# Attention scores by rows in two of every three units, with the reciprocal sums applied per head after the output projection

## The chip, the cores and the metric

The kernel runs on one core of a Trainium2 chip. The metric is the device time of one execution in microseconds (us). The median of 3 runs of the kernel before is 1313.21 us (1313.07 to 1313.99). All times inside the kernel come from one profiled execution.

The engines are called as in the profile: PE multiplies matrices, PEld is its load of the stationary operand, DVE is the vector engine, ACT computes the exponential and the GELU, POOL and SP do little arithmetic and issue transfers. PSUM is the memory into which PE writes; a bank holds 512 float32 values in each of 128 partitions.

## The reference, cut to what matters

The block is an attention with cached keys and values, followed by a gated MLP, each behind a modulated layer norm. The change touches the attention:

```python
q = (x @ wq).reshape(B, Sq, Hq, Dh).transpose(0, 2, 1, 3)   # Sq 2048, Hq 32, Dh 128
k = jnp.repeat(k_cache, rep, axis=1)                       # 8 key heads, rep 4
v = jnp.repeat(v_cache, rep, axis=1)
scores = jnp.einsum('bhqd,bhkd->bhqk', q, k) * Dh ** (-0.5)
p = softmax(scores, axis=-1)
o = jnp.einsum('bhqk,bhkd->bhqd', p, v)
return o.transpose(0, 2, 1, 3).reshape(B, Sq, Hq * Dh) @ wo  # wo: 4096 x 512
```

The result is scaled by a gate and added to x; a second layer norm and the MLP follow, which multiplies one half of its hidden values with a 2048 x 2048 spatial projection of the other half.

## The kernel before, in words

The attention is cut into 128 units. Unit u belongs to group g = u // 16 (one key head with its four query heads) and to query tile j = u % 16 (128 queries). The main loop runs over iterations `it`, and each iteration over eight slots. In iteration `it` the program computes the scores of unit `it` (`qk`), the product of P and V of an earlier unit (`pv_at` says in which iteration), and the output projection of a still earlier one (`wo_at`). The instructions are written out in this order by hand, so each engine runs its own in the order of the loop. Work that has a due time is put in by `at(iteration, slot, function)`: it comes first in its slot. `fill` holds the matmuls of the query projection, four in each iteration, in slots 0 to 3.

There are two ways to compute a unit.

- **By columns**: `qk` makes the scores transposed, keys in the partitions, so that the exponential lands in `pT` as PV needs it. `pv` takes 128 x 128 pieces of `pT` as the stationary operand and V with a column of ones as the moving one (129 columns, 64 matmuls in a unit). The column of ones yields the sum of the row; DVE takes its reciprocal and multiplies (`onorm`, L1091 and L1092), and a transposing transfer on SP turns the result into `oT` (L1100).
- **By rows** (`by_rows(u)`): the queries are in the partitions. ACT's exponential sums up the row as it goes (`accum_out`, L1012). `turn_rows` adds the two half sums, takes the reciprocal, multiplies the 128 x 2048 rows of P by it on DVE (L1050), and issues a transposing transfer on SP that writes them into `pT` (L1051), one for each of the four heads. `pv_rows` then has V as the stationary operand and 512 columns of `pT` as the moving one (16 matmuls in a unit), and its result is `oT` after one copy (L1068).

Before the change the even units from 8 (`TURN_A`) to 124 are computed by rows, 59 of them; their PV comes three iterations after their scores, and that of the 69 others one iteration after. There is one PV in each iteration, except in iteration 9, which has none, and iteration 127, which has two.

`wo_proj` multiplies the four heads of `oT` with `wo` in one PSUM bank, four matmuls that accumulate, and DVE adds the bank to `xacc` (L1125; in the first group a copy, L1123). In the last group (units 112 to 127) DVE then multiplies by the gate (L1130), adds x (L1131) and takes the statistics (L697, L698) of the second layer norm. `ln2` puts the rest in: the square root on POOL in the next iteration, the normalisation `xn` and its transposing transfer `xnT` on SP in slot 4, and the modulated `hT` (L1156) in slot 5 of the iteration after that. From iteration 128 on the MLP's first matmuls fill the slots (`zrun`), and DVE takes the statistics of their GELU (`z2_stats`, L1312) and normalises it (`z2_norm`); the spatial matmuls (L1456) need all of that.

PSUM has two banks each under the names `o_ps` (PV) and `misc` (query projection and output projection) and two pairs under `s_ps` (scores). A bank is taken again when the engine that empties it is done. `pT` has three homes (`pT0`, `pT1`, `wsp`), given out by the table before the loop. The rows of P lie in six buffers (`pn`), taken in turn. For each group g from 1 on, SP loads the keys with a transposing transfer in iteration 16 (g - 1) + 11, slot 5; POOL loads V and the two weights after it has seen that the transposes of a certain row unit have landed (`after_rows`).

Of the kernel before, what the change touches and what calls it, by code (L numbers as in the profile page):

```python
# [15 lines left out]
P = 128  # L16
# [559 lines left out]
def kernel(  # L576
# [118 lines left out]
    def ln_stats(mv, j, src):  # L695
        st = stat.tile([P, 1, nc.vector.BN_STATS_DIM], FP32, name="bnst")
        nc.vector.bn_stats(out=st[:, 0, :], in_=src)  # L697
        nc.vector.bn_aggr(out=mv[:, j, :], in_=st[:])  # L698
# [266 lines left out]

    TURN_A, TURN_B = 2 * CT, NU - 2

    def by_rows(u):
        return TURN_A <= u < TURN_B and u % 2 == 0

    def pv_at(u):
        return u + 3 if by_rows(u) else u + 1

    def wo_at(u):
        return pv_at(u) + (3 if u < TURN_B - CT else 2)
# [11 lines left out]
    def at(it, slot, fn):  # L987
        later.setdefault((it, slot), []).append(fn)

    def qk(u, i):  # L990
# [10 lines left out]
        if by_rows(u):  # L1001
            hh, half = divmod(i, 2)
            for c in range(2):
                k0 = (2 * half + c) * 512
                nc.tensor.matmul(  # L1005
                    s_ps[:, c * 512 : (c + 1) * 512],
                    lhsT=qTs[b][:, hh, jj * P : (jj + 1) * P],
                    rhs=groups[g]["kT"][:, k0 : k0 + 512],
                    start=True,
                    stop=True,  # L1010
                )
            nc.scalar.activation(  # L1012
                out=rows_of(u, hh)[:, half * HK : (half + 1) * HK],
                in_=s_ps[:],
                func=ACT.Exp,
                scale=inv_sqrt_dh,
                accum_out=rsums[u][:, i : i + 1],
            )
            if half == 1:
                at(*divmod(u * NSLOT + i + 2, NSLOT), lambda: turn_rows(u, hh))  # L1020
            return
        for h in range(2):
            kt = 2 * i + h
# [12 lines left out]
        )  # L1036

    def rows_of(u, hh):
        return pn[((u - TURN_A) // 2 * REP + hh) % len(pn)][:, 0:SK]

    def turn_rows(u, hh):
        c0 = u * REP + hh
        rs, rinv = rsums[u], rall[:, c0 : c0 + 1]
        tot = stat.tile([P, 1], FP32, name="tot")
        nc.vector.tensor_tensor(  # L1045
            out=tot[:], in0=rs[:, 2 * hh : 2 * hh + 1], in1=rs[:, 2 * hh + 1 : 2 * hh + 2], op=ALU.add
        )
        nc.vector.reciprocal(out=rinv, in_=tot[:])  # L1048
        rows = rows_of(u, hh)
        nc.vector.tensor_scalar(out=rows, in0=rows, scalar1=rinv, scalar2=None, op0=ALU.mult)  # L1050
        nc.sync.dma_start_transpose(out=pTs[u][:, :, hh * P : (hh + 1) * P], in_=rows)  # L1051

    def pv_rows(u, i, n):

# [48 lines left out]

    def wo_proj(u):
        g, j = divmod(u, NT)
        ps = {}

        def mm(hh):
            if hh == 0:
                ps[0] = bank("misc")  # L1110
            X_ps = ps[0]
            nc.tensor.matmul(  # L1112
                X_ps[:],
                lhsT=oTs[u][:, hh, :],
                rhs=groups[g]["wo"][:, hh, :],
                start=(hh == 0),
                stop=(hh == REP - 1),
            )
            if hh < REP - 1:
                return  # L1120
            if g == 0:
                xaccs[j] = late.tile([P, D], FP32, name=f"xacc{j}", bufs=1)
                nc.vector.tensor_copy(out=xaccs[j][:], in_=X_ps[:])  # L1123
            else:
                nc.vector.tensor_tensor(  # L1125
                    out=xaccs[j][:], in0=X_ps[:], in1=xaccs[j][:], op=ALU.add
                )
            if g == HKV - 1:
                xa = xaccs[j]
                nc.vector.tensor_tensor(out=xa[:], in0=xa[:], in1=ga_rows[:], op=ALU.mult)  # L1130
                nc.vector.tensor_tensor(  # L1131
                    out=x_sb[:, j, :], in0=xa[:], in1=x_sb[:, j, :], op=ALU.add
                )
                ln_stats(mv2, j, x_sb[:, j, :])

        return [lambda hh=hh: mm(hh) for hh in range(REP)]

# [127 lines left out]
    for g in range(1, HKV):  # L1265
        it = (g - 1) * NT
        at(it + 11, 5, lambda g=g: load_k(g))
        loads = (
            lambda g=g: load_v(g),
            lambda g=g: load_wq(g, nc.gpsimd),  # L1270
            lambda g=g: load_wo(g, nc.gpsimd),
        )
        for k, load in enumerate(loads):
            if g == 1:
                at(5, 0, load)
                continue
            u = next(u for u in range(it + 4 + 2 * k, NU) if by_rows(u))
            at(u + 1, 5, lambda u=u: after_rows(u))
            at(u + 1, 5, load)

# [92 lines left out]
    for it in range(NU + 6):  # L1373
# [3 lines left out]
        elif it == NU:  # L1377
            free_a.close()
            z2p = fast.enter_context(tc.tile_pool(name="z2p", bufs=1))
            zs["z2"] = z2p.tile([P, NT, FH], BF16, name="z2")  # L1380
        pvs = [u for u in (it - 5, it - 3, it - 1) if 0 <= u < NU and pv_at(u) == it]
        wos = [u for u in range(max(it - 6, 0), min(it - 2, NU)) if wo_at(u) == it]
        wf = [fn for u in wos for fn in wo_proj(u)]
        for i in range(NSLOT):
            for fn in later.pop((it, i), []):
# [190 lines left out]
```

## Time and profile before

| what | value |
|---|---|
| median of 3 runs | 1313.21 us |
| profiled execution, span from first to last instruction | 1311.5 us |
| granted PE clock, mean | 0.999 |
| score matmuls by columns (L1024) and by rows (L1005) | 1104 and 944 |
| PV matmuls by columns (L1080) and by rows (L1059) | 4416 and 944 |
| transfers: row transposes (L1051), oT (L1100) | 236 and 69 |
| POOL waits in `seen` (L1258) | 18 |

The time of a run has about 1.7 us around the span. A page of the profile lists the busy time of each engine, the span in 40 slices of 32.8 us with the busy share in tenths, the chain of work that ended last followed back through its releasers, and groups of instructions with their count, busy time, mean duration in ns and the idle time of their engine just before them. An answer of the trace by windows gives the busy time of each engine in a stretch, with the number of instructions behind it. Mean durations of matmuls are from start to the modelled end; since they are pipelined, what one costs is the distance from start to start.

### The profile page before, as it was taken

What the parts mean: (1) busy time and instruction counts of PE and PEld (TensorE: products, weight loads), DVE (VectorE), ACT (ScalarE), POOL (GpSimd) and SP (SyncE); (2) the same over time, 40 slices, a digit from 0 to 9 for tenths busy, and PEclk for the clock granted to TensorE, in tenths of its full rate; (3) what the DMA queues carried; (4) which work ended last, traced back from release to release, by engine and by line L of the source; (5) the groups of instructions that cost most, each with busy time, mean ns of one, the idle gap of its engine ahead of it and who ended that gap; (6) DMA issues with size and microseconds to landing.
All of it is one profiled execution on the core that took longest, in us unless ns stands there. A gap on an engine that the chain in (4) does not pass through costs nothing.

```text
span 1311.5 us, 24369 instructions
## 1 busy us (share of the span) xinstructions
PE 1303.8 (99%) x9527; PEld 736.9 (56%) x9527; DVE 689.5 (53%) x1693; ACT 1113.0 (85%) x1533; POOL 59.4 (5%) x115
## 2 busy tenths in 40 slices
PE   9999999999999999999999999999999999999998
PEld 5665555555555555555555555555555555644445
DVE  5644455444454544444445454444445588784444
ACT  7899999999999999999999999999999999550000
POOL 1200000000000000000000000000000011120000
PEclk9999999999999999999999999999999999999999
DMA  6669778877897677867886778668876688364300
GB/s 181 154 97 157 130 128 154 158 118 133 158 166 149 121 144 155 144 125 140 160 169 122 133 157 156 125 127 153 175 143 125 118 140 144 103 133 96 82 21 27
DMA packets 607723, 174.45 MB, mean 133 GB/s; under 512 B 597264, under 2 KB 603664, under 8 KB 607600
## 3 DMA queue, kind: packets, MB, share of 16 engines
q1 hardware_dynamic: 600576, 153.67, 64.9%
q0 software_dynamic: 4432, 16.91, 4.1%
q10 hardware_dynamic: 2592, 2.23, 0.5%
q8 instruction: 77, 1.26, 0.4%
q14 instruction: 46, 0.38, 0.1%
HBM read 21.89 MB, written 2.10 MB: 18 GB/s over the span
## 4 chain that ended last, share of the span: by engine, by line
PE 96%; DVE 2%; DMA 1%; POOL 0%; issue 0%; ACT 0%; DVEq 0%; POOLq 0%
PE o_ps L1080 19%; PE s_ps L1024 18%; PE s_ps L1005 16%; PE o_ps L1059 16%; PE misc L1112 8%; PE misc L945 8%; PE misc L1456 7%; PE s_ps L1290 1%; PE o_ps L1477 1%; DVE stz L1312 1%; PE s_ps L1477 1%; DMA xnT<-xn 0%; DMA wmod_a<-in_w_mod_dram 0%; DVE z L686 0%; POOL rstd_lnz L682 0%; PE misc L855 0%
## 5 line engine op out<-in xcount | busy, mean ns | idle before, releaser
L1031 ACT ACTIVATE pT<-s_ps 128x1024 bf16<-128x1024 f32 x552 | 561.1, 1025 | 30.7 <-PE s_ps L1024 8.7
L1080 PEld LDWEIGHTS <-pT 128*128 128x128 bf16 x4416 | 295.3, 98 | 128.9
L1080 PE MATMUL o_ps<-v,pT 128*128 128x129 bf16 x4416 | 339.7, 220 | 0.0
L1024 PE MATMUL s_ps<-qT,kT 128*128 128x512 bf16 x1104 | 328.1, 379 | 0.3 <-ACT pT L1031 0.2
L1005 PE MATMUL s_ps<-kT,qT 128*128 128x512 bf16 x944 | 280.7, 379 | 0.0
L1012 ACT ACTIVATE win_sb<-s_ps 128x1024 bf16<-128x1024 f32 x238 | 243.7, 1025 | 3.5
L1112 PE MATMUL misc<-wo_g,oT 128*128 128x512 bf16 x512 | 194.0, 379 | 0.0
L945 PE MATMUL misc<-hT,wq_g 128*128 128x512 bf16 (+2 forms) x520 | 187.0, 371 | 0.1
L1024 PEld LDWEIGHTS <-kT 128*128 128x128 bf16 x1104 | 107.3, 98 | 114.9 <-issue 2.3
L1012 ACT ACTIVATE pn<-s_ps 128x1024 bf16<-128x1024 f32 x156 | 159.6, 1024 | 2.0 <-ACT wmod_a L1012 0.3
L1059 PEld LDWEIGHTS <-v 128*128 128x128 bf16 x944 | 92.4, 98 | 111.4
L956 DVE CAST qT<-misc 128x512 bf16<-128x512 f32 x125 | 85.7, 686 | 122.8 <-PE misc L945 122.8
L1068 DVE CAST oT<-o_ps 128x512 bf16<-128x512 f32 x59 | 40.8, 692 | 194.9 <-PE o_ps L1059 194.9
L1059 PE MATMUL o_ps<-wsp,v 128*128 128x512 bf16 x480 | 142.1, 379 | 0.0
L1059 PE MATMUL o_ps<-pT,v 128*128 128x512 bf16 x464 | 138.0, 379 | 0.0
L1005 PEld LDWEIGHTS <-qT 128*128 128x128 bf16 x944 | 92.2, 98 | 61.6
L1045 DVE TENSOR_TENSOR tot<-rs 128x1 f32<-128x1 f32 x236 | 36.4, 154 | 127.1 <-ACT win_sb L1012 84.8
L1456 PE MATMUL misc<-wsp,z 128*128 128x512 bf16 (+2 forms) x560 | 101.4, 336 | 0.2
L1050 DVE TENSOR_SCALAR win_sb<-win_sb,rall 128x2048 bf16<-128x2048 bf16 x119 | 89.7, 753 | 4.4 <-DVE rall L1048 0.3
L1012 ACT ACTIVATE wmod_a<-s_ps 128x1024 bf16<-128x1024 f32 x78 | 79.9, 1025 | 0.0
L1456 PEld LDWEIGHTS <-z 128*128 128x128 bf16 x560 | 50.5, 98 | 49.4 <-DVE z L686 1.6
L1125 DVE TENSOR_TENSOR xacc<-misc,xacc 128x512 f32<-128x512 f32 x112 | 76.2, 680 | 0.0
(110 smaller groups left out, 824.1 us busy)
## 6 DMA issues: line engine op xcount, KB each, us to landing
v<-in_A_v_cache_dram POOLq DMA_DIRECT2D x7, 512.0 KB, 6.6
wq_g<-in_A_wq_dram POOLq DMA_DIRECT2D x7, 512.0 KB, 3.9
wo_g<-in_A_wo_dram POOLq DMA_DIRECT2D x7, 512.0 KB, 4.5
wsp<-in_w_mod_dram POOLq DMA_DIRECT2D x1, 2048.0 KB, 9.1
out_dram<-yout ACTq DMA_DIRECT2D x16, 128.0 KB, 1.7
win_sb<-in_B_w_in_dram POOLq DMA_DIRECT2D x1, 1792.0 KB, 8.0
x_sb<-in_A_x_dram SPq DMA_DIRECT2D x3, 512.0 KB, 6.1
oT<-onorm SPq DMA_TRANSPOSE x69, 2.8
```

Of the source, the lines that this page charges most:

```text
L945: nc.tensor.matmul(ps[0][:, o0 : o0 + n], lhsT=wqs[g][:, dt, hh * DH : (hh + 1) * DH], rhs=hTs[ch][:, dt, c0 : c0 + n], start=(dt == 0), s ...
L956: nc.vector.tensor_copy(out=dst, in_=src)
L1005: nc.tensor.matmul(s_ps[:, c * 512 : (c + 1) * 512], lhsT=qTs[b][:, hh, jj * P : (jj + 1) * P], rhs=groups[g]["kT"][:, k0 : k0 + 512], sta ...
L1012: nc.scalar.activation(out=rows_of(u, hh)[:, half * HK : (half + 1) * HK], in_=s_ps[:], func=ACT.Exp, scale=inv_sqrt_dh, accum_out=rsums[u ...
L1024: nc.tensor.matmul(s_ps[:, h * 512 : (h + 1) * 512].rearrange("p (r q) -> p r q", r=REP), lhsT=groups[g]["kT"][:, kt * P : (kt + 1) * P], ...
L1031: nc.scalar.activation(out=pTs[u][:, 2 * i : 2 * i + 2, :], in_=s_ps[:].rearrange("p (k q) -> p k q", k=2), func=ACT.Exp, scale=inv_sqrt_dh,)
L1050: nc.vector.tensor_scalar(out=rows, in0=rows, scalar1=rinv, scalar2=None, op0=ALU.mult)
L1059: nc.tensor.matmul(o_pss[u][:], lhsT=groups[g]["v1"][:, kt, 0:DH], rhs=pTs[u][:, kt, :], start=(kt == 0), stop=(kt == NKT - 1),)
L1080: nc.tensor.matmul(o_ps[:, hh % 2, 0 : DH + 1], lhsT=pTs[u][:, kt, hh * P : (hh + 1) * P], rhs=groups[g]["v1"][:, kt, 0 : DH + 1], start=( ...
L1112: nc.tensor.matmul(X_ps[:], lhsT=oTs[u][:, hh, :], rhs=groups[g]["wo"][:, hh, :], start=(hh == 0), stop=(hh == REP - 1),)
L1125: nc.vector.tensor_tensor(out=xaccs[j][:], in0=X_ps[:], in1=xaccs[j][:], op=ALU.add)
L1456: nc.tensor.matmul(g_ps[:, :n], lhsT=z2[:, st, f * P : (f + 1) * P], rhs=wsp[t][:, st, c0 : c0 + n], start=(st == 0), stop=(st == NT - 1 a ...
```

## The change

Two of every three units from 8 to 125 are computed by rows, 79 in place of 59. With `(u - 8) % 3` the remainders 0 and 1 are by rows; their PV comes 2 and 3 iterations after their scores, that of remainder 2, by columns, 1 iteration after. There is still one PV in each iteration (none in 9, two in 127).

The rows of P are no longer multiplied by the reciprocal. They are turned as they are, one slot earlier than before (`i + 1` for `i + 2`), and the transfer is issued ahead of the sum and the reciprocal, which stay.

The reciprocals are applied to the projected output. For a row unit each of the four heads gets a bank of its own in `wo_proj`, with one matmul that starts and stops, and DVE adds the bank times the head's reciprocal to `xacc` (`scalar_tensor_tensor`; in the first group's first head a `tensor_scalar`). A column unit keeps one bank and one addition. The unit after whose transposes V and the weights are loaded must now be the second row unit of a pair.

```diff
--- before.py
+++ after.py
@@ -965,11 +965,15 @@
 
     TURN_A, TURN_B = 2 * CT, NU - 2
 
+    LAGS = (2, 3, 1)
+
     def by_rows(u):
-        return TURN_A <= u < TURN_B and u % 2 == 0
+        return TURN_A <= u < TURN_B and (u - TURN_A) % len(LAGS) < len(LAGS) - 1
+
+    row_units = [u for u in range(NU) if by_rows(u)]
 
     def pv_at(u):
-        return u + 3 if by_rows(u) else u + 1
+        return u + (LAGS[(u - TURN_A) % len(LAGS)] if by_rows(u) else 1)
 
     def wo_at(u):
         return pv_at(u) + (3 if u < TURN_B - CT else 2)
@@ -1017,7 +1021,7 @@
                 accum_out=rsums[u][:, i : i + 1],
             )
             if half == 1:
-                at(*divmod(u * NSLOT + i + 2, NSLOT), lambda: turn_rows(u, hh))
+                at(*divmod(u * NSLOT + i + 1, NSLOT), lambda: turn_rows(u, hh))
             return
         for h in range(2):
             kt = 2 * i + h
@@ -1036,19 +1040,19 @@
         )
 
     def rows_of(u, hh):
-        return pn[((u - TURN_A) // 2 * REP + hh) % len(pn)][:, 0:SK]
+        return pn[(row_units.index(u) * REP + hh) % len(pn)][:, 0:SK]
 
     def turn_rows(u, hh):
         c0 = u * REP + hh
-        rs, rinv = rsums[u], rall[:, c0 : c0 + 1]
+        rs = rsums[u]
+        nc.sync.dma_start_transpose(
+            out=pTs[u][:, :, hh * P : (hh + 1) * P], in_=rows_of(u, hh)
+        )
         tot = stat.tile([P, 1], FP32, name="tot")
         nc.vector.tensor_tensor(
             out=tot[:], in0=rs[:, 2 * hh : 2 * hh + 1], in1=rs[:, 2 * hh + 1 : 2 * hh + 2], op=ALU.add
         )
-        nc.vector.reciprocal(out=rinv, in_=tot[:])
-        rows = rows_of(u, hh)
-        nc.vector.tensor_scalar(out=rows, in0=rows, scalar1=rinv, scalar2=None, op0=ALU.mult)
-        nc.sync.dma_start_transpose(out=pTs[u][:, :, hh * P : (hh + 1) * P], in_=rows)
+        nc.vector.reciprocal(out=rall[:, c0 : c0 + 1], in_=tot[:])
 
     def pv_rows(u, i, n):
 
@@ -1103,35 +1107,49 @@
 
     def wo_proj(u):
         g, j = divmod(u, NT)
+        each = by_rows(u)
         ps = {}
 
+        def into(first, X_ps, scale):
+            if first:
+                xaccs[j] = late.tile([P, D], FP32, name=f"xacc{j}", bufs=1)
+            xa = xaccs[j]
+            if scale is None and first:
+                nc.vector.tensor_copy(out=xa[:], in_=X_ps[:])
+            elif scale is None:
+                nc.vector.tensor_tensor(out=xa[:], in0=X_ps[:], in1=xa[:], op=ALU.add)
+            elif first:
+                nc.vector.tensor_scalar(
+                    out=xa[:], in0=X_ps[:], scalar1=scale, scalar2=None, op0=ALU.mult
+                )
+            else:
+                nc.vector.scalar_tensor_tensor(
+                    out=xa[:], in0=X_ps[:], scalar=scale, in1=xa[:], op0=ALU.mult, op1=ALU.add
+                )
+
         def mm(hh):
-            if hh == 0:
+            if hh == 0 or each:
                 ps[0] = bank("misc")
-            X_ps = ps[0]
             nc.tensor.matmul(
-                X_ps[:],
+                ps[0][:],
                 lhsT=oTs[u][:, hh, :],
                 rhs=groups[g]["wo"][:, hh, :],
-                start=(hh == 0),
-                stop=(hh == REP - 1),
-            )
-            if hh < REP - 1:
+                start=(hh == 0 or each),
+                stop=(hh == REP - 1 or each),
+            )
+            if each:
+                c0 = u * REP + hh
+                into(g == 0 and hh == 0, ps[0], rall[:, c0 : c0 + 1])
+            elif hh == REP - 1:
+                into(g == 0, ps[0], None)
+            if hh < REP - 1 or g < HKV - 1:
                 return
-            if g == 0:
-                xaccs[j] = late.tile([P, D], FP32, name=f"xacc{j}", bufs=1)
-                nc.vector.tensor_copy(out=xaccs[j][:], in_=X_ps[:])
-            else:
-                nc.vector.tensor_tensor(
-                    out=xaccs[j][:], in0=X_ps[:], in1=xaccs[j][:], op=ALU.add
-                )
-            if g == HKV - 1:
-                xa = xaccs[j]
-                nc.vector.tensor_tensor(out=xa[:], in0=xa[:], in1=ga_rows[:], op=ALU.mult)
-                nc.vector.tensor_tensor(
-                    out=x_sb[:, j, :], in0=xa[:], in1=x_sb[:, j, :], op=ALU.add
-                )
-                ln_stats(mv2, j, x_sb[:, j, :])
+            xa = xaccs[j]
+            nc.vector.tensor_tensor(out=xa[:], in0=xa[:], in1=ga_rows[:], op=ALU.mult)
+            nc.vector.tensor_tensor(
+                out=x_sb[:, j, :], in0=xa[:], in1=x_sb[:, j, :], op=ALU.add
+            )
+            ln_stats(mv2, j, x_sb[:, j, :])
 
         return [lambda hh=hh: mm(hh) for hh in range(REP)]
 
@@ -1274,7 +1292,7 @@
             if g == 1:
                 at(5, 0, load)
                 continue
-            u = next(u for u in range(it + 4 + 2 * k, NU) if by_rows(u))
+            u = next(u for u in range(it + 4 + 2 * k, NU) if by_rows(u) and not by_rows(u + 1))
             at(u + 1, 5, lambda u=u: after_rows(u))
             at(u + 1, 5, load)
 
@@ -1378,8 +1396,8 @@
             free_a.close()
             z2p = fast.enter_context(tc.tile_pool(name="z2p", bufs=1))
             zs["z2"] = z2p.tile([P, NT, FH], BF16, name="z2")
-        pvs = [u for u in (it - 5, it - 3, it - 1) if 0 <= u < NU and pv_at(u) == it]
-        wos = [u for u in range(max(it - 6, 0), min(it - 2, NU)) if wo_at(u) == it]
+        pvs = [u for u in range(max(it - 5, 0), min(it, NU)) if pv_at(u) == it]
+        wos = [u for u in range(max(it - 8, 0), min(it, NU)) if wo_at(u) == it]
         wf = [fn for u in wos for fn in wo_proj(u)]
         for i in range(NSLOT):
             for fn in later.pop((it, i), []):
```

## The prediction

> **What bounds the kernel now.** I read the page from the top: engine shares, then the tenths by slice, then the chain that ended last.
>
> ```profile
> PE 1303.8 (99%) x9527; PEld 736.9 (56%) x9527; DVE 689.5 (53%) x1693; ACT 1113.0 (85%) x1533; POOL 59.4 (5%) x115
> ...
> DVE  5644455444454544444445454444445588784444
> ...
> PE 96%; DVE 2%; DMA 1%; POOL 0%; issue 0%; ACT 0%; DVEq 0%; POOLq 0%
> ```
>
> The chain is PE from end to end. DVE sleeps half the time, except in slices 32 to 35 (1049 to 1180 us), where it is at 7 to 9 tenths. Both facts carry the forecast: the change takes a little from PE everywhere and gives DVE work just there.
>
> The windows view gives stretches of that last part and, first, two neighbouring iterations of the steady state (unit 68 scored by rows, unit 69 by columns). Its columns: length, then busy time of PE, PEld, DVE, ACT, POOL, clock, DMA share, GB/s.
>
> ```profile
> 601.38:610.18 8.80, 8.80 (x89) 5.97 (x88) 5.62 (x15) 8.71 (x16) 0.00 (x0) 1.00 0.43 81
> 610.18:618.82 8.64, 8.64 (x42) 3.92 (x41) 2.88 (x8) 8.11 (x10) 0.17 (x2) 1.00 0.97 178
> 1105.81:1114.62 8.81, 8.81 (x89) 5.98 (x88) 7.79 (x17) 8.22 (x9) 2.23 (x5) 1.00 0.78 111
> 1146.15:1184.30 38.15, 38.09 (x184) 17.80 (x182) 31.92 (x85) 21.67 (x22) 9.12 (x14) 1.00 0.65 125
> ```
>
> PE is full in all of them. An iteration costs 8.81 or 8.64 us according to the unit whose PV it runs, not the one that it scores: eight slots, each with two score matmuls, one projection matmul, and either eight 129-column matmuls (PV of a column unit) or two of 512 (PV of a row unit).
>
> **1. PE gains 3.2 us.** By the timeline, PE's slot is 1.101 us with column PV and 1.079 with row PV; eight slots differ by 0.173 us. Row units go from 59 to 79 (u from 8 to 125, two of three), so 20 iterations change. Rows scoring beside row PV, new, has the same five 512-column matmuls in a slot: 1.079. From iteration 13 to 123 column PV is in 55 before and 37 after: 18 x 0.173 = 3.1; iteration 126 changes as well: 0.2. Iterations 8 to 12 lack their projections and are paced by ACT (1.005 us a slot by rows, 0.915 by columns, in the timeline at 81 to 98 us); one more of them is scored by rows. Slot by slot they come to 8.64 + 7.69 + 8.16 + 8.21 + 8.14 = 40.84 us, after 8.64 + 7.48 + 8.48 + 7.91 + 8.26 = 40.77 before: +0.1. ACT stays cover elsewhere: 2 x 8 x 1.005 + 8 x 0.915 = 23.4 us in three iterations, against PE's 8.81 + 2 x 8.63 = 26.1.
>
> On this term the Trainium skill, page "TensorE: Matmul & The Clock Gate", section "Back-to-back issue gap", speaks otherwise: streamed pairs of load and matmul go at about 81 ns for 128 columns and 131 ns for 512. By that the estimate is 64 x 81 - 16 x 131 = 3.1 us a unit, 62 us in all. The trace shows 56.6 and 215.8 ns, so it has no part in the sum.
>
> **2. The removed multiply gives nothing.** The page's groups have it (L1050, with two more of its kind, and below it the drain that term 4 uses):
>
> ```profile
> L1050 DVE TENSOR_SCALAR win_sb<-win_sb,rall 128x2048 bf16<-128x2048 bf16 x119 | 89.7, 753 | 4.4 <-DVE rall L1048 0.3
> ...
> L1125 DVE TENSOR_TENSOR xacc<-misc,xacc 128x512 f32<-128x512 f32 x112 | 76.2, 680 | 0.0
> ```
>
> 236 x 0.753 us go from DVE, hidden under PE: 0. The add and the reciprocal stay, one slot earlier. A transpose need not wait for them, only for ACT's second half.
>
> **3. More transposes, less time for them: +1.8 us (0 to 4).** Row transposes go from 236 to 316, those of oT from 69 to 49. The DMA view of 600 to 740 us:
>
> ```profile
> GB/s 33 24 200 208 185 28 170 157 180 187 100 176 205 211 176 32 172 205 211 173 172 34 201 217 173 24 38 200 210 166 28 41 200 210 120 75 44 202 212 172
> ...
> pT<-win_sb SPq DMA_TRANSPOSE x8, 4.4
> ...
> kT<-in_A_k_cache_dram SPq DMA_TRANSPOSE x1, 5.6
> ```
>
> One of 0.524 MB lands 4.4 us after issue; at the 205 to 210 GB/s of full slices, each next one 2.5 us later. Three iterations need 8 x 2.5 + 0.6 = 20.6 us of 26.1: enough. What is tight is the first row unit of a pair, whose PV now starts two iterations after its scores. From its own start, its heads are ready at 2.9, 5.1, 7.4 and 9.5 us; SP must first issue the column unit's oT, which waits for onorm (9.4) and takes 1.6, so the fourth issues at 11.1 and lands at 15.5. PV wants it at 8.81 + 8.63 + 0.43 = 17.87: slack 2.4. The V and weight loads start about at this unit's start, in idle DMA time; the V load before delayed a transpose by 0.9 to 1.8 us: covered. Not covered is a K transpose in SP's queue between the heads, in iterations 11, 59 and 107: it holds SP 2.2 to 3.6 us and pushes the landing to about 18.2. PE then stands 1.3 us in iteration 13 (short iterations before it) and 0.4 at the two others: 2.1, of which I take 1.8. In the last group an xnT transpose comes ahead of the second head in SP's queue and waits for DVE until 5.9: 0.8, inside the slack. The six row buffers cost no wait: the seventh head of a pair is written from 13.7 on, and the first, whose buffer it takes, has landed at 7.3.
>
> The Trainium skill, page "DMA: Bandwidth & Descriptors", section "Latency and other measured facts", gives 261 GB/s for a DMA transpose; a transpose would then take 2.0 us, an estimate, and this term would be 0. The full slices of this trace don't reach it.
>
> **4. Four drains for one.** A row unit's projection now fills a bank per head, each emptied by a scalar_tensor_tensor. The trace has none. Below: 0.68 us (L1125: same tiles without the scalar); above: two passes, 1.37. I take 0.70, nearest to L1125; 0.72 from start to start, as the chain below runs.
>
> In ordinary iterations this is free: misc has two banks, the third matmul needs the first drain two slots (2.16 us) later, and DVE has 3 us to spare. From unit 112 on a finish (L1130, L1131, statistics) follows; 3.0 us from drain to end:
>
> ```profile
> 1106.41 0.68 DVE L1125 TENSOR_TENSOR xacc<-misc,xacc 128x512 f32<-128x512 f32 x1
> 1107.12 0.69 DVE L1130 TENSOR_TENSOR xacc<-xacc,ga_rows 128x512 f32<-128x512 f32 x1
> 1107.85 0.69 DVE L1131 TENSOR_TENSOR x_sb<-xacc,x_sb 128x512 bf16<-128x512 f32 x1
> 1108.58 0.69 DVE L697 BATCH_NORM_STATS2 bnst<-x_sb 128x6 f32<-128x512 bf16 x1
> 1109.31 0.18 DVE L698 BATCH_NORM_AGGREGATE mv<-bnst 128x2 f32<-128x6 f32 x1
> ```
>
> With one projected unit per iteration DVE then has 9.0 us at most, 24.6 in three iterations of 26.1, and my schedule shows no bank late. It breaks in two places.
>
> **Iteration 126: +3.7 us (2.5 to 4.5).** It projects units 120 and 122, now both row units: eight banks in eight slots. DVE begins it with unit 121's drain and finish (0.82 to 3.82 us) and unit 125's sums (to 4.14), so the first drain ends at 4.83. The third matmul wants that bank at 3.02 and starts at 4.90: 1.88 lost. Unit 120's finish runs to 9.4, then 0.35 of xn and a drain to 10.44: the seventh matmul, due at 9.22, starts at 10.5: 1.28. After hT (0.9) and a drain to 12.05 the eighth, due at 11.58, starts at 12.1: 0.52. DVE's backlog of 4 us dies in iteration 127, where it idles 4.6 before.
>
> **Iterations 128 and 129: +2.7 us (1.5 to 4).** Units 123 and 125 bring three drains more each. The first three fit in an idle 1.6 us but for 0.4; the next, 3 x 0.72 = 2.2, find DVE with no gap from 1134.7 to 1160.7. That chain sets the end of this phase:
>
> ```profile
> DVE hT L1156 <- DMA xnT<-xn: 4.0, 1, 4.0
> ...
> PEld L1456 <- DVE z L686: 1.6, 4, 0.6
> ```
>
> These waits (1100 us to the end) say that DVE's one idle time there waits for a transpose which itself waits for DVE, and that PE's spatial matmuls already wait for the last normalised z. So 0.4 + 2.2 = 2.6, with a bank wait 2.7, goes into the end. PE loses about 2.5 in iteration 129 for the same banks; it runs beside and is not added.
>
> **Sum**, against the span of 1311.5 us: -3.2 + 1.8 + 3.7 + 2.7 = +5.0, so 1316.5. The median run is 1313.2, 1.7 above the span: 1318.2, rounded to **1318**.
>
> **Rivals.**
> - Faster: PE's gain stands and neither banks nor DMA cost anything, because DVE reaches the drains sooner than I schedule (it would have to regain 1.9 us by iteration 126): 1313.2 - 3.2 = 1310. For: DVE is 53% busy. Against: its four slices at 7 to 9. 0.12.
> - Half of it: one of the two places is absorbed or half as large: about 1313 to 1315. 0.18.
> - DMA as the bound: past 3.1 us a transpose (2.4 us of slack over four) each of 39 pairs stalls; at 3.3 that is 39 x 0.8 = 31 us: 1344. For: transposes, unlike before, queue through two iterations on end. Against: full slices at 205 GB/s. 0.05.
> - Dear drains: past 1.1 us each, the next query projection finds its bank late in all 79 units; at 1.37, 0.8 each, 63 us: 1376. 0.03.
> - Column PV paced by its weight loads: 98 ns each (PEld L1080 in the groups), so 64 x 98 - 16 x 215.8 ns = 2.8 us a unit, 56 in all: 1257. Against: its matmuls start 56.6 ns apart. 0.01. The stream prices of the Trainium skill's page (term 1) are the same thought.
>
> That the rows aren't selected as said is no rival: which units they are is plain arithmetic in the diff.
>
> **Chances and range.** A run of this kernel tells 0.2% (2.6 us) from no change. Forecast (+2.7 to +10): 0.61. Faster: 0.12 + 0.01. Within 0.2%: 0.18. Slower: 0.61 + 0.08 = 0.69. The range takes the forecast's own bounds and the half case, 1311.5 to 1324; the faster rival and the two dear ones stay outside.
>
> **What will show it.** Term 1: iteration starts 8.81, 8.64, 8.64 us apart, and 3136 matmuls of 129 columns instead of 4416. Term 3: PE waits on a row transpose only after K loads; if in every pair, the DMA rival. Term 4: PE waits of some 4 us in iteration 126 for DVE's drain, of 2 in 129, and z's normalisation later against the end of the last PV; drains of 0.7 us. No such waits would make the forecast wrong to the fast side.

## The result, and the profile after

The changed kernel takes **1360.62 us** (median of 6 runs, 1356.88 to 1371.76) beside 1313.05 (6 runs, 1312.90 to 1313.99) of the kernel before on the same chip: 1.0377 times as long, with a 95% interval of 1.0349 to 1.0406. The forecast was 1318, with a range up to 1324. The direction was right and the size was not. The runs also spread over 1.1%, where those of the kernel before agree within 0.1%: what costs here does not fall alike each time.

The profiled execution is the shortest of the six, with a span of 1355.0 us, 43.5 more than before. Its page, with the lines that answer to those shown ahead of the prediction, and two more (the clock granted to TensorE and the busy share of the DMA engines, in tenths):

```profile
PE 1314.2 (97%) x8567; PEld 696.9 (51%) x8567; DVE 704.2 (52%) x1794; ACT 1116.2 (82%) x1693; POOL 54.7 (4%) x115
...
DVE  6532545444554554355544554455435688894444
PEclk9999999999999999899999999999989999999999
DMA  7679899999999999999899999998999999364300
...
PE 88%; DMA 7%; DVE 2%; ACT 2%; issue 1%; POOL 0%; SPq 0%; ACTq 0%; DVEq 0%
```

PE was 96% of the chain that ends last and is 88% now; DMA's share went from 1% to 7%. The DMA engines are at nine tenths nearly throughout, and two slices of PEclk fall to 8. The waits of PE say for what it stands:

```profile
PE o_ps L1063 <- DMA wsp<-wmod_a: 8.9, 5, 4.4
PE o_ps L1063 <- DMA wsp<-win_sb: 6.9, 5, 3.9
PE misc L1133 <- DVE xacc L1126: 5.7, 5, 2.1
PE o_ps L1063 <- DMA wsp<-pn: 5.4, 3, 3.8
PE o_ps L1063 <- issue: 4.0, 2, 2.8
```

L1063 is PV of a row unit (`pv_rows`), and the tile that it waits for is the transposed P (its buffer is called wsp; behind the arrow stands the buffer of the rows). The columns are the sum, the number and the longest wait. 21.2 us go to row transposes that land late. The 4.0 us marked "issue" have no releaser in the profile; they stand at the same place, before the first PV of a pair, and I count them with the others: 25.2 us. In the kernel before not one PV had such a wait. L1133 is the wo projection: its 5.7 us are the waits for a drained bank that term 4 foresaw.

Where no transpose is late, the iterations are as the prediction has them. The windows of iterations 68 and 69 (the length is the first figure), and last that of iteration 76, with a late one:

```profile
619.41:628.22 8.81, 8.81 (x90) 5.98 (x88) 3.42 (x12) 8.72 (x16) 0.00 (x0) 1.00 0.65 122
628.22:636.85 8.63, 8.63 (x41) 3.91 (x40) 5.15 (x16) 8.62 (x17) 0.00 (x0) 1.00 1.06 197
690.70:704.76 14.06, 10.27 (x41) 4.16 (x40) 4.45 (x9) 8.24 (x10) 0.00 (x0) 0.88 1.07 201
```

Iteration 76 is 5.4 us too long, in two parts. PE is busy for 10.27 us of 14.06, so it stands 3.79. And its own work takes 1.64 us more than the 8.63 of its neighbour, since the granted clock is 0.88 in the mean: it is 0.5 for 3.4 us.

To place all of it I compare the start of each iteration (its first exponential) in the two traces, and count what an iteration has over the undisturbed 8.81, 8.63, 8.63:

| stretch | us against before |
|---|---|
| up to iteration 13 (1.6 of it is there at iteration 5, ahead of every changed unit) | +1.8 |
| iterations 13 to 126, undisturbed | -3.4 |
| late transposes, with the slow clock behind them, iterations 13 to 125 | +37.5 |
| iteration 126 (waits for banks) | +3.9 |
| from iteration 127 to the end (196.2 before, 200.0 now) | +3.8 |
| sum | +43.6 |

The 37.5 are 25.2 of waits, 10.2 of half clock (20.5 us at 0.5), and small rests. One of these is a wait of 0.75 us in iteration 75 for an exponential of ACT, which itself waited 1.24 us until a late transpose had read the row buffer that it writes; the prediction had said that the six row buffers cost no wait. The 37.5 fall on few iterations: 13 (4.6 us), 28 (3.1), 61 (6.6), 76 (5.5), 109 (7.5), and 58, 94 and 106 (1.4 to 1.8 each) hold 32 of them; 23 of the 39 pairs have none over 0.35 us.

One such case, from the start of the pair 74 and 75. First GpSimd's timeline, then that of SP's queue; columns are start, duration, and the issue. A long duration in SP's queue means that the issue itself is held up.

```profile
674.61 0.76 POOL L721 DMA_DIRECT2D wq_g<-in_A_wq_dram  x1 [0.30 <-issue]
675.37 0.18 POOL L1276 COPY seen<-pT 1x1 bf16<-1x1 bf16 x1
675.49 0.75 POOL L739 DMA_DIRECT2D wo_g<-in_A_wo_dram  x1
```

```profile
675.16 4.95 SPq L1048 DMA_TRANSPOSE wsp<-win_sb  x1
680.16 6.55 SPq L1048 DMA_TRANSPOSE wsp<-wmod_a  x1
686.80 1.85 SPq L1048 DMA_TRANSPOSE wsp<-pn  x1
```

The two weight loads and the first head's transpose go out within 0.9 us. The DMA view of 660 to 690 us shows when each landed, counted from its issue (last figure):

```profile
wo_g<-in_A_wo_dram POOLq DMA_DIRECT2D x1, 512.0 KB, 11.5
...
wsp<-win_sb SPq DMA_TRANSPOSE x1, 12.1
```

Before, these took 4.5 and 4.4 us. The second head can be issued only at 680.16, the third at 686.80, and PV of this unit starts 3.79 us late:

```profile
695.02 1.03 PE L1063 MATMUL o_ps<-wsp,v 128*128 128x512 bf16 x2 [3.79 <-DMA wsp<-pn]
```

The DMA engines are not moving data at their full rate all that time. In the DMA view of 676 to 686 us (40 slices of 0.25 us) the rate falls while both kinds of transfer are in flight:

```profile
DMA  7699799599996000799999989999932234649989
GB/s 98 164 197 262 279 295 295 229 327 266 114 63 41 33 16 14 160 290 291 300 272 41 58 29 61 40 253 291 105 54 70 53 47 92 84 83 267 250 198 329
```

In the 14th to 16th slice, from 679.25 us, almost nothing moves (14 to 33 GB/s) and the engines are idle, with both kinds of transfer still to land. In the 22nd to 26th slice, from 681.25 us, the engines are busy for eight or nine tenths and move 29 to 61 GB/s; in the 29th to 36th they move 47 to 105, and from the 30th are busy for only two to six tenths. Over these 10 us the mean is 160 GB/s. The prediction's view of the kernel before had 200 to 217 in slices full of row transposes.

### The profile page after: what moved, and what is told of

Its sections match the earlier page's. It is cut to its first block, busy times and chain, and to the rows that moved or that the text cites. A ratio compares the mean times of both kernels' runs of the same rounds, so it can differ in the third digit from the quotient of the medians.

```text
span 1355.0 us, 22644 instructions
## 1 busy us (share of the span) xinstructions
PE 1314.2 (97%) x8567; PEld 696.9 (51%) x8567; DVE 704.2 (52%) x1794; ACT 1116.2 (82%) x1693; POOL 54.7 (4%) x115
## 4 chain that ended last, share of the span: by engine, by line
PE 88%; DMA 7%; DVE 2%; ACT 2%; issue 1%; POOL 0%; SPq 0%; ACTq 0%; DVEq 0%
PE s_ps L1009 19%; PE o_ps L1063 19%; PE o_ps L1084 12%; PE s_ps L1028 11%; PE misc L945 8%; PE misc L1474 7%; PE misc L1133 7%; DMA wsp<-win_sb 3%; PE s_ps L1347 2%; DMA wsp<-wmod_a 2%; PE s_ps L1308 1%; PE o_ps L1495 1%; DMA wsp<-pn 1%; ACT win_sb L1016 1%; DMA wsp<-in_w_mod_dram 1%
## 5 line engine op out<-in xcount | busy, mean ns | idle before, releaser
L1035 ACT ACTIVATE pT<-s_ps 128x1024 bf16<-128x1024 f32 x392 | 398.0, 1024 | 65.8 <-PE s_ps L1028 49.8
L1009 PE MATMUL s_ps<-kT,qT 128*128 128x512 bf16 x1264 | 376.1, 379 | 0.8 <-ACT win_sb L1016 0.8
L1016 ACT ACTIVATE win_sb<-s_ps 128x1024 bf16<-128x1024 f32 x318 | 325.1, 1024 | 4.2 <-DMA wsp<-win_sb 1.2
L1126 DVE SCALAR_TENSOR_TENSOR xacc<-misc,rall,xacc 128x512 f32<-128x512 f32 x310 | 231.9, 748 | 54.4 <-PE misc L1133 47.4
L1084 PEld LDWEIGHTS <-pT 128*128 128x128 bf16 x3136 | 209.6, 98 | 91.1
L1084 PE MATMUL o_ps<-v,pT 128*128 128x129 bf16 x3136 | 241.2, 220 | 0.0
L1028 PE MATMUL s_ps<-qT,kT 128*128 128x512 bf16 x784 | 236.1, 383 | 0.4 <-ACT pT L1035 0.2
L1063 PE MATMUL o_ps<-wsp,v 128*128 128x512 bf16 x640 | 194.2, 387 | 25.4 <-DMA wsp<-wmod_a 8.9
L1063 PEld LDWEIGHTS <-v 128*128 128x128 bf16 x1264 | 123.3, 98 | 180.3 <-issue 29.8
L1016 ACT ACTIVATE pn<-s_ps 128x1024 bf16<-128x1024 f32 x208 | 212.7, 1023 | 2.0 <-PE s_ps L1009 0.4
L1133 PE MATMUL misc<-wo_g,oT 128*128 128x512 bf16 x512 | 194.7, 380 | 5.7 <-DVE xacc L1126 5.7
L1063 PE MATMUL o_ps<-pT,v 128*128 128x512 bf16 x624 | 185.7, 379 | 0.0
L945 PEld LDWEIGHTS <-wq_g 128*128 128x128 bf16 x528 | 50.9, 99 | 39.8 <-issue 3.1
```

Source lines behind the costliest of these rows:

```text
L945: nc.tensor.matmul(ps[0][:, o0 : o0 + n], lhsT=wqs[g][:, dt, hh * DH : (hh + 1) * DH], rhs=hTs[ch][:, dt, c0 : c0 + n], start=(dt == 0), s ...
L1009: nc.tensor.matmul(s_ps[:, c * 512 : (c + 1) * 512], lhsT=qTs[b][:, hh, jj * P : (jj + 1) * P], rhs=groups[g]["kT"][:, k0 : k0 + 512], sta ...
L1016: nc.scalar.activation(out=rows_of(u, hh)[:, half * HK : (half + 1) * HK], in_=s_ps[:], func=ACT.Exp, scale=inv_sqrt_dh, accum_out=rsums[u ...
L1028: nc.tensor.matmul(s_ps[:, h * 512 : (h + 1) * 512].rearrange("p (r q) -> p r q", r=REP), lhsT=groups[g]["kT"][:, kt * P : (kt + 1) * P], ...
L1035: nc.scalar.activation(out=pTs[u][:, 2 * i : 2 * i + 2, :], in_=s_ps[:].rearrange("p (k q) -> p k q", k=2), func=ACT.Exp, scale=inv_sqrt_dh,)
L1063: nc.tensor.matmul(o_pss[u][:], lhsT=groups[g]["v1"][:, kt, 0:DH], rhs=pTs[u][:, kt, :], start=(kt == 0), stop=(kt == NKT - 1),)
```

## The experiments

Times of the kernel before, on the chip of each set of runs, were 1312.9 to 1313.4. "Stands" are PE's, counted as in the table above, for iterations 13 to 125 and with the clock's share. The theories are numbered as in the expectations. **Theory 1**: the loads of K, V and the weights now fall where a pair of row units has little slack, and cost by their place. **Theory 2**: 316 row transposes are simply too many for the DMA engines. **Theory 3**: the cost is the keys' transpose, which holds SP's queue. **Theory 4** came from the first runs: a load and row transposes that are in flight together slow each other down far more than by sharing a rate.

### All loads left out

From group 2 on, every group takes its tiles from group 1:

```diff
+    def same_group():
+        for g in range(2, HKV):
+            groups[g], wqs[g] = groups[1], wqs[1]
+    at(12, 0, same_group)
...
+        if g > 1:
+            continue
```

> This kernel leaves out the loads of keys, V and both weights for the groups from 2 on (group 1's tiles are used again); all other work, the row transposes included, is that of the changed kernel. Theory 1 (loads): of the 41 us that PE stands between iterations 13 and 126 of the changed kernel, 37 are waits for row transposes that share the DMA engines or SP's queue with the loads of the next group. Without the loads only iteration 13 (the load of group 1's keys, 4.6 us) and the bank waits at the end stay: 1313 - 3 + 4.6 + 7.6 = 1322 us, between 1317 and 1325. Theory 2 (rate): 316 row transposes are by themselves too many for the DMA engines in two iterations on end; then PE still stands in most pairs and the time stays above 1340 us.

Measured: 1322.93 us (1321.18 to 1326.94), ratio 1.0080 (1.0056 to 1.0104). All the row transposes are there, and PV waits 2.5 us in iteration 13 (group 1's K is still loaded there) and 0.3 and 0.4 in 121 and 124:

```profile
PE o_ps L1067 <- issue: 2.9, 2, 2.5
```

The time is close to the 1322 that theory 1 gave. Theory 2 falls, and with it the rival that had DMA as the bound.

### Loads at other places

First V and the weights behind the first unit of a pair; then also three units apart, and K in a column unit's iteration:

```diff
-            u = next(... if by_rows(u) and not by_rows(u + 1))
+            u = next(... if by_rows(u) and by_rows(u + 1))
```

> V and the weights are loaded after the first row unit of a pair has landed, not after the second, so that the loads meet the transposes of the second unit, whose PV comes an iteration later. The keys' load stays where it is. Theory 1: the waits in iterations 25, 40, 43, 46, 58, 73 to 76, 88, 91, 94 and 106 (17 us in the profile) go, those of the key loads (13, 28, part of 61 and 109, 12 to 18 us) stay: 1335 to 1346 us, against 1357 to 1372 for the changed kernel. Theory 3 (SP's queue): nearly all is the key transpose that holds SP's queue; then little changes, above 1350 us.

```diff
-        at(it + 11, 5, lambda g=g: load_k(g))
+        k_it = next(i for i in range(it + 12, NU) if not by_rows(i))
+        at(k_it, 1, lambda g=g: load_k(g))
...
-            u = next(u for u in range(it + 4 + 2 * k, NU) if by_rows(u) and not by_rows(u + 1))
+            u = next(u for u in range(it + 4 + 3 * k, NU) if by_rows(u) and by_rows(u + 1))
```

> V and the weights as in the run before, but three units apart; the keys' transpose goes to slot 1 of a column unit's iteration (from iteration 16 (g - 1) + 12 on), behind the pair's last transpose in SP's queue and well ahead of the next pair's first. Nothing is left out and nothing is cheaper. Theory 1: all waits for row transposes go, what stays is the gain of PE (-3) and the bank waits of iterations 126 and 129 (+7.6): 1316 to 1320 us. Theory 2: above 1340 us. Theory 3: as theory 1 here.

Measured: 1353.02 us (1351.04 to 1356.07, ratio 1.0306) and 1347.45 (1342.91 to 1350.75, ratio 1.0253). Both expectations missed: the stands only moved to other iterations, 33 and 24 us in all. So it isn't enough to move the loads to another unit of the pair. In both kernels every one of the 16 loads from iteration 20 to 125 whose landing is in the trace was in flight with row transposes; the loads landed after 8.9 and 8.8 us in the mean, and the transposes beside them after 7.8 and 7.9 (at most 15.9), against 4.9 for the other transposes. That gave theory 4.

### One bank for a row unit's projection

Row units go through the projection as column units do:

```diff
-        each = by_rows(u)
+        each = False
```

> Leaves out the multiplication by the reciprocals for row units: their four heads accumulate in one bank with one addition, as column units do. All else, loads and transposes too, is the changed kernel. Drains as the cause of the end's loss: iteration 126 goes back from 12.5 to 8.6 us and the time from the start of iteration 127 to the end from 200.6 to 196.9: 7.6 us less than the changed kernel, with the waits for transposes (37 us, scattering by some us from run to run) as they were: 1349 to 1361 us. If the drains also load DVE in ordinary iterations, more than 12 us go. If nothing goes, the banks are not the cause.

Measured: 1351.56 us (1348.04 to 1353.82, ratio 1.0289). The wait in iteration 126 is gone (3.9 us), and the stretch from iteration 127 to the end is 198.1 us, against 200.0 and 196.2 before. Of these 198.1 us, 1.7 are a PV that waits for a late row transpose in iteration 127. The stands at transposes remain, 39.3 us. The drains cost about what term 4 said and have no part in the rest.

### The kernel before, with its loads among transposes

```diff
-        ... in_=pTs[u][0:1, NKT - 1, 511:512])
+        ... in_=pTs[u][0:1, NKT - 1, 127:128])
```

The first index is in the last head's quarter of P transposed, the second in the first head's: GpSimd then lets a load go while three transposes are still to come.

> The kernel before, unchanged but for one index: GpSimd's V and weight loads wait for the transpose of a row unit's first head instead of its last, so that they are issued while the other heads' transposes are still to come. Theory 4 (a GpSimd load and row transposes in flight together slow each other down far more than by sharing): the loads and the transposes beside them land 10 to 13 us after their issue, against 4.4 and about 4.5 before, and some iterations near the loads stand; time between 1313 and 1325, since this kernel's P V comes three iterations after its scores. Plain sharing of a rate (theory 2): each lands in at most 7 us, and nothing stands: 1313.

Measured: 1313.15 us (1312.38 to 1314.36), ratio 1.0001 (0.9990 to 1.0011). The DMA view of 215 to 960 us, of this kernel:

```profile
wo_g<-in_A_wo_dram POOLq DMA_DIRECT2D x6, 512.0 KB, 9.3
v<-in_A_v_cache_dram POOLq DMA_DIRECT2D x5, 512.0 KB, 7.7
wq_g<-in_A_wq_dram POOLq DMA_DIRECT2D x5, 512.0 KB, 7.0
```

The weights that landed after 4.5 and 3.9 us now take 9.3 and 7.0; the 34 transposes beside loads take 7.2 in the mean and up to 14.1. Some are slower than the 7 us that I had put as the most by plain sharing, but the mean is below the 10 to 13 us that I expected. No iteration stands for it, since PV comes three iterations after the scores here. So the slow transfers don't need the changed kernel. The kernel before was spared them by its gate and by the idle stretch of DMA that each column unit left, and it could have borne them.

### The old pattern with the rest of the change

```diff
-    LAGS = (2, 3, 1)
+    LAGS = (3, 1)
```

> The changed kernel with the old pattern of units: every second unit by rows, P V three iterations later; the unnormalised turn one slot earlier and the drains per head stay, and the loads keep their gate. Theory 4 and also theory 1: the 37 us of waits for transposes are gone; what is left over the kernel before is the banks' waits of iteration 126 (about 2 us with fewer row units) and of the end (about 2.2 to 3.8): 1315 to 1318. If the drains or the early turn were what costs: 1330 or more.

Measured: 1318.21 us (1317.31 to 1318.97), ratio 1.0040 (1.0025 to 1.0056). That is just above the 1315 to 1318 that I expected. No PV waits for a transpose. Iteration 126 is 1.3 us longer than before (PE waits 1.1 us for a bank), and 197.8 us follow on the start of iteration 127. From iteration 13 to 126 the time is that of the kernel before, 983.8 us: the early turn without the multiply buys nothing there and costs nothing. The drains per head cost some 3 us.

### One gap for each group

One unit of each group that would be the second of its pair is scored by columns. K is loaded in its iteration, and V and the weights behind K: all of them fall in the one stretch without row transposes. First with the last eight units by columns, then with rows up to the end.

```diff
+    gaps = {
+        g: next(u for u in range((g - 1) * NT + 6, NU) if u > TURN_A and (u - TURN_A) % 3 == 1)
+        for g in range(1, HKV)
+    }
     def by_rows(u):
-        return TURN_A <= u < TURN_B and (u - TURN_A) % len(LAGS) < len(LAGS) - 1
+        if not TURN_A <= u < NU - 8 or u in gaps.values():
+            return False
+        return (u - TURN_A) % len(LAGS) < len(LAGS) - 1
...
+        at(gaps[g], 1, lambda g=g: load_k(g))
```

> The changed kernel with one gap a group: one row unit of each group is computed by columns, at its old place, and K, then V and the weights (behind K) are loaded in the stretch without row transposes that this makes; and the last eight units are computed by columns, so that no drain per head falls at the end. 68 row units against 59 before. Theory 4: no waits for transposes and none for banks: before less 9 times 0.173 us, 1311 to 1312. If it is the share of transposes in all that sets the waits (theory 2): 1330 or more.

> As the run before with the gaps, but rows up to the last units, as in the changed kernel: 72 row units. Theory 4: less four conversions more, plus the banks' waits of iteration 126 (3.9) and of the end (3.8): 1317 to 1319. Theory 2: 1335 or more.

The first: 1313.83 us (1312.45 to 1315.21), ratio 1.0003 (0.9993 to 1.0012). With 68 row units, 9 more than before, PV waits 2.1 us for transposes, in three waits, where it waited 25.2. The time, though, was expected 2 us lower: it is the same as before. From iteration 13 to 127 eight more row units are worth 8 x 0.173 = 1.4 us, of which 0.9 go to a wait in iteration 13 and 0.3 remain (992.3 us for that stretch, against 992.6); iterations 10 and 11 are 0.55 longer. So the conversion is worth about what it costs to begin it.

The second: 1327.59 us (1326.46 to 1328.95), ratio 1.0107 (1.0092 to 1.0122), against 1317 to 1319: missed by 9. The middle behaves (3.2 us of stands). The end takes 206.0 us from iteration 127 on, against 200.0 in the changed kernel. There GpSimd's load of B's first weights, issued at 1113.43, meets the last row transposes: one lands 10.2 us after its issue, PV waits 2.9 us, and half a clock of 3.4 us follows. I had cleared the loads of A alone. It is again a load beside a transpose, but for the most part not a fall of the rate: this load has 1.8 MB, and from 1116.2 to 1120 us the DMA engines move 328 to 466 GB/s.

### K alone, V and the weights alone

The first of the two keeps K's loads only, the second those of V and the weights:

```diff
+            if g > 1:
+                at(it + 4, 0, lambda g=g: same_loads(g))
+                break
```

```diff
     def load_k(g):
+        if g > 1:
+            groups.setdefault(g, {})["kT"] = groups[1]["kT"]
+            return
```

> The changed kernel with GpSimd's V and weight loads of groups 2 to 7 left out (they reuse group 1's tiles), K's transposes by SP kept where they are. Theory 4 (what costs is a GpSimd load in flight together with row transposes): as without any loads, 1322 to 1327, with no wait over 2.6 us behind iteration 13 but the banks' one at 126. If K's transposes, which stand in the same queue as the rows' and hold them up, are what costs: 1340 or more.

> The changed kernel with K's loads of groups 2 to 7 left out (they reuse group 1's keys), GpSimd's V and weight loads kept where they are. Theory 4: nearly all of the waits stay, 1348 to 1362. The rival, K in the transposes' queue: 1330 or less.

Measured: 1326.70 us (1325.59 to 1327.28, ratio 1.0104) with K alone, 1352.53 (1348.22 to 1353.90, ratio 1.0303) with V and the weights alone. The waits of PV with K alone (L1067 there):

```profile
PE o_ps L1067 <- issue: 2.4, 1, 2.4
PE o_ps L1067 <- DMA wsp<-win_sb: 1.6, 1, 1.6
PE o_ps L1067 <- DMA wsp<-wmod_a: 1.4, 1, 1.4
...
PE o_ps L1067 <- DMA wsp<-pn: 0.2, 1, 0.2
```

The three long ones are in iterations 13, 61 and 109, the three that the prediction named for K's transposes; the fourth is 0.2 us in iteration 121. In all the stands are 7.8 us, against 31.5 with V and the weights alone. With neither there were 3.6, with both 37.5: the parts nearly add up (3.6 + 4.2 + 27.9 = 35.7). Theory 3 falls with this: K alone is the small part.

### The same loads from other queues

V and the weights of groups 2 to 7 issued by SP, in the queue of the transposes, and then by ScalarE's queue (there in slot 2 of the next pair's first iteration, where GpSimd's had been):

```diff
-            nc.gpsimd.dma_start(out=v1[:, :, 0:DH], in_=v_dram[:, g])
+            (nc.gpsimd if g == 1 else nc.sync).dma_start(out=v1[:, :, 0:DH], in_=v_dram[:, g])
...
-            at(u + 1, 5, lambda u=u: after_rows(u))
```

> The changed kernel with V and the weights of groups 2 to 7 issued by SP, behind the transposes of a pair's second unit, in place of GpSimd: the same bytes at nearly the same place, in the transposes' own queue. If it is the two queues in flight together that slow each other: the transposes land in 4 to 7 us, little stands, 1322 to 1332. If copies and transposes slow each other from whichever queue: transposes beside a load still land in 8 to 12 us, 1345 or more.

> The changed kernel with V and the weights of groups 2 to 7 issued by ScalarE's queue in the third slot of the next pair's first iteration, where GpSimd issued them in the changed kernel: a second queue beside the transposes' own, but not GpSimd's. If any second queue in flight beside the transposes slows both: transposes beside a load land in 8 to 12 us and the time stays at 1345 to 1362. If it takes GpSimd's queue: they land in 5 to 7 us and the time comes near that of the loads by SP, 1325 to 1334.

Measured: 1327.60 us (1326.52 to 1328.54, ratio 1.0107) by SP; 1340.59 (1336.62 to 1346.24, ratio 1.0222) by ScalarE. With SP, the waits of PV are near those with K alone:

```profile
PE o_ps L1063 <- issue: 3.9, 2, 2.9
PE o_ps L1063 <- DMA wsp<-wmod_a: 2.4, 3, 1.4
PE o_ps L1063 <- DMA wsp<-win_sb: 1.9, 1, 1.9
```

The same bytes, and 33 us of the 47.6 are back. ScalarE's queue lies between, 27 against 15 and 48 us over the kernel before, and its expectation of either end missed. But these two runs change the queue and the place at once: SP doesn't wait for a landing, so that its loads go out further ahead of the next pair's first transpose. The transfers, for iterations 20 to 125 (means, longest in brackets; up to 70 of a trace's 210 to 280 row transposes and two of its 18 loads have no landing in the trace). The second column is the time from a load's issue to that of the next pair's (or row unit's) first transpose, negative where the transpose went out first:

| loads by | first transpose behind it, us | loads land after, us | transposes in flight over 0.5 us with a load | the other transposes |
|---|---|---|---|---|
| GpSimd, in idle stretches (before) | 2.6 to 3.7 | 5.0 (7.1) | 19: 4.9 (6.2) | 4.6 |
| GpSimd, old pattern with the rest of the change | 2.0 to 3.3 | 4.9 (6.8) | 15: 5.6 (6.8) | 4.8 |
| GpSimd, among transposes (before, gate moved) | one went out 0.1 to 1.4 ahead of each load | 8.5 (13.4) | 34: 7.2 (14.1) | 4.7 |
| GpSimd (the change) | -0.9 to 2.0 | 6.6 (11.5) | 16: 8.1 (12.1) | 4.9 |
| ScalarE | 0.7 to 1.1 | 5.1 (10.4) | 18: 6.3 (8.5) | 5.0 |
| SP | 1.6 to 4.6 | 5.1 (7.9) | 18: 5.3 (7.1) | 4.9 |
| GpSimd, in the gaps (68 row units) | 6.7 and more | 6.6 (7.7), three at once | 1: 4.5 | 4.9 |

GpSimd's loads in the old pattern, two to three us ahead of the next transpose, are nearly as harmless as SP's. At like places the queues differ little: transposes issued 1 to 2 us after a single load (no other load within 3 us) took 6.8 us beside GpSimd's (15, in five traces), 5.9 beside ScalarE's (9) and 6.7 beside SP's (2). So the distance in time goes with most of the difference, and a share of the queue itself is not shown.

None of these versions beats the kernel before; the one with short gaps equals it.

## Why the prediction was wrong

**The step that failed is in term 3**: "The V and weight loads start about at this unit's start, in idle DMA time: covered." They do start there, 2.2 to 3.8 us into the pair's first iteration for the weights. But the time isn't idle any more: the pair before has its last transpose landing up to 2.9 us into that iteration, which is what GpSimd's gate waits for, and the pair's own first transpose goes out at 2.87 us. I had seen a V load delay a transpose by 0.9 to 1.8 us in the trace before, and took that as the price of an overlap. It was the price of a load that goes out 2.6 us or more ahead of the transpose. Term 3 was +1.8 (0 to 4) and measures 37.5, half clock included. About 28 of that are GpSimd's loads, shown by leaving them out.

**K, within term 3.** The three places were right, and the sizes were too small: 1.3 and 0.4 twice were predicted; the kernel with K alone has waits of 2.4, 1.6 and 1.4, and a half clock behind the first makes its iteration 4.2 us longer. I had used 4.4 us for a transpose; with queued neighbours those without a load beside them take 4.9.

**Term 1 was right**: 8.81, 8.63 and 8.63 us, 3136 matmuls of 129 columns, and -3.4 us from iteration 13 to 126 for a forecast of -3.3 there. **Term 2 was right**: the multiply gave nothing.

**Term 4 was right in its places and nearly in its sizes.** The new drain (L1126) takes 748 ns in the mean of 310, where I put 700. Iteration 126 lost 3.9 us (3.7 predicted), in the three waits that the schedule named, of 1.37, 1.71 and 0.31 us. The longer one in PE's timeline:

```profile
1152.63 0.38 PE L1133 MATMUL misc<-wo_g,oT 128*128 128x512 bf16 x1 [1.71 <-DVE xacc L1126]
```

The end lost 3.8 (2.7 predicted). PE waits 2.1 us for a bank in iteration 129, as forecast, and 3.4 us of half clock follow. With V and the weights alone and with the loads by ScalarE the same wait is there without a half clock, and the end takes 198.7 and 199.2 us, 2.5 and 3.0 over before. So the half clock, which the prediction didn't have, is about what lies beyond its 2.7. Whether those 2.7 come by DVE's chain, as it said, or by PE's own wait, no run separates.

**The rivals.** Two came about as near in time, and neither has this mechanism. Dear drains (1376, with a chance of 0.03) needed more than 1.1 us a drain, and one takes 0.75. DMA as the bound (1344, 0.05) had every pair stall at too low a rate, and 23 of 39 pairs don't stall. With the loads gone or in gaps, the same transposes keep up. What I lacked was a rival in which the added transposes take the idle stretch that something else had been using.

**What stays open.** That GpSimd's loads and row transposes slow each other when they go out close together is shown; why isn't, and neither is a part of the queue. The prediction set a higher rate for transposes aside because the full slices of its view don't reach it. That holds for slices of 3.5 us; in the 18th to 20th slice of the view of 676 to 686 us nearly all is transposes, at 290 to 300 GB/s. The Trainium skill, page "Trainium Kernel Development and Optimization", section "Key Constraints", says that DMAs from SP, ACT and POOL run on the same 16 DMA engines and interleave, so that several issuers save no more than issue time. Interleaving at an unchanged total rate is not what the trace shows: 160 GB/s over those 10 us and stretches of 14 to 105, against 200 to 217 with the transposes alone.

## What to carry to other kernels

An idle stretch of a shared resource may be the slot of a transfer that is gated into it, so before a change fills such stretches, list every transfer that starts there and price it as if it ran against the new work, not at its old latency. The lag between a producer and a consumer hides slow transfers: with its gate moved, the kernel before bore transposes of up to 14 us with a lag of three iterations, and the change cut the lag to two at the same time as it took the idle stretch. Where a load must run near DMA transposes, let it go out behind the last of one stretch and two us or more ahead of the next (by SP, without a gate, this took back 33 us here), or make one stretch free for all loads.

## What the runs showed of the hardware

A 0.5 MB load by GpSimd and row transposes by SP that went out close together landed after up to 15 and 16 us, and SP's next issue took up to 12 us. In the kernel before loads take 4 to 7 and transposes 4 to 6; without the loads SP's issue takes 4.2 us at most. How close matters: in six traces, 36 transposes issued up to 1 us ahead of a single load by GpSimd took 9.4 us in the mean (6.8 to 14.1), and 36 issued 2 to 4 us ahead of one took 5.1 (4.4 to 7.9).

A wait of PE can cost more than itself. Between 60 and 1250 us, over all 14 traces, each of the 17 waits of 2.9 us or more between matmuls came with 3.4 or 6.8 us of a granted clock of 0.5; of the 27 waits of 2.0 to 2.9 us 9 did, and of all those between 1 and 2 us one. A slot of 1.08 us then takes 2.11, and a wait of 3.8 us cost 5.4. The Trainium skill, page "TensorE: Matmul & The Clock Gate", section "Part 1: The HAM clock gate (the "warmup" mystery)", has a free-running window of about 3.4 us, after one idle one of which the clock is halved. The length agrees, and a window that runs free would leave it to chance which waits are hit. But a wait need not fill a window: one of 2.1 us was followed by a half clock in four of the traces.
